# Element order of the PSUM copies of transposed q and k in a sparse-attention and mixture-of-experts kernel

## The chip, the core and the metric

The kernel runs on one core of a Trainium2 chip. The metric is the device time of one execution, in microseconds. A core has a matrix engine (TensorE, PE in the tables; its weight loads are listed as PEld), a vector engine (VectorE, DVE), an activation engine (ScalarE, ACT), GpSimd (POOL) and a queue for transfers (SyncE, SP). They run side by side and wait for one another through semaphores. PE writes its results to PSUM; DVE and ACT copy them from there to SBUF, from which PE reads its operands.

## The reference

Eight batches of eight heads, 576 positions, 64 features. Heads 0 to 3 see the 32 latest positions (local), heads 4 to 7 see the earlier positions that are equal modulo 32 (strided). The attention's output, as 4608 tokens of 512 features, goes through a top-1 mixture of eight experts with a capacity of 80 tokens.

```python
scores = scale * np.matmul(q, k.transpose(0, 1, 3, 2))
mask_local = (rel >= 0) & (rel < stride)                     # stride = 32
mask_strided = (rel >= 0) & (pos[None, :] % stride == pos[:, None] % stride)
scores = np.where(masks[None, :, :, :], scores, -1000000000.0)
attn = softmax(scores); attn_out = np.matmul(attn, v)
x = attn_out.transpose(0, 2, 1, 3).reshape(B * S, H * D)
expert_idx = np.argmax(x @ w_gate, axis=1)                   # gate_w: its probability
# of an expert's tokens the 80 with the largest gate are kept
h = np.maximum(x[tok_idx] @ w1[e], 0.0)
out[tok_idx] = gate_w[tok_idx, None] * (h @ w2[e])
```

## The kernel before

The attention takes up most of the first 235 us. Its work comes in 32 items: for each batch two of the local heads and two of the strided heads. In step i the kernel computes the scores of item i, the exponentials and their sums of item i-1, and the products with the values of item i-2. It transposes a q or a k for a later item, splits one chunk of expert weights into two float16 parts, and carries the previous batch's logits and rows of x on. So four steps make a batch. Each of these pieces is a generator, and `weave` takes their steps in an order that the table `WIN` sets. The instructions of each engine then stand in exactly that order: nothing is moved later by a scheduler, and an engine that waits holds up all that is queued behind it.

q and k arrive with nine positions side by side in a partition's row. PE transposes them in nine pieces of 128x128 (line 332), three to a PSUM tile `tp`; a piece j holds the positions 9 s + j. A copy per tile (two for k, one for each half of the partitions) puts them where the products read them: `qt` and `ktl` for local heads, `qs` and `kst` for strided ones, with positions in their natural order. Before the change the copy runs over pieces, then over positions of a piece, so that it reads PSUM without steps and writes every ninth float. The halves of `ktl` and `kst` that belong to other heads hold zeros, so that one product serves two.

Which engine makes a copy is told by the table `EV`, with "a" for ACT and "v" for DVE: the key `k01` is the middle tile of a local k, `k11` that of a strided k, `q..` those of q, all of them on ACT. In the profile the copies are lines 288 (ACT, plain), 290 (ACT, times a constant) and 292 (DVE).

For local items the weights (`pl`) are transposed (line 420), copied to `ptl` and multiplied with the values `vlo` (line 430). For strided items the weights `pr` become `pts`, and the products with the values (line 460) give a PSUM tile `o` with 288 columns, whose copy goes to `xr` (in the last batches to a part of `cp` or `raw`). There are two such copies an item, one per residue pair `rr`; before the change each holds all four heads of one residue and writes every fourth float. DVE reduces the scores' maxima (line 345), subtracts them (346), sums the exponentials that ACT makes (400, sums in 404) and takes half of the weight splits (211, after ACT's half in 210). GpSimd multiplies the weights by the reciprocal sums (407).

Of the kernel before, what the change touches and what calls it, by code (L numbers as in the profile page):

```python
# [20 lines left out]
P = 128  # L21
# [4 lines left out]
NTL = S // 32            # query tiles of a local head, 32 queries against 64 keys  # L26
NQ = 96                  # partitions of a batch's rows of x, 6 tokens each
NC6 = S // NQ
NSEG = 16                # segments of tokens in the routing, 8 experts each
NCAND = 16               # candidates kept of a segment and expert  # L30
SLOTS = 80               # tokens of an expert in the fast path
NEG = -1e30
FAR = 1000000.0
SC = 16.0                # scale of float16 parts
HALF = 4096              # a half of an expert's weights (w1 or w2), per partition
# [3 lines left out]
NR = 2                   # staged chunks during the attention  # L39
NST = 8                  # and after it  # L40
TL = ((0, 5), (5, 9))    # pairs of tiles of a local item
NPRE = 5                 # halves split during the attention
# [9 lines left out]
def moe_attention(ctx: ExitStack, tc, q, k, v, wg, w1, w2, cap, out):  # L52
# [3 lines left out]
    # rows of x by token id plus one; row 0 is zeros  # L56
    xs = dram.tile([NT + 1, DM], F32, name="xs")

# [8 lines left out]
    # additive masks; local: rows (head of the pair, tile parity, query), columns keys from 32 before the tile's  # L67
    # first query; strided: rows (head, block), columns blocks
    # their storage holds the routing's candidates later
# [32 lines left out]
    # column n of gates holds tokens 576 * (n // 6) + 6 * p + n % 6; chunk j of a partition's row of g288 holds column  # L102
    # 16 j + segment, so that position i of the row holds token 6 i + tb[j] - 1
# [6 lines left out]
    def attention_constants():  # L110
        nc.gpsimd.memset(mstr, 0.0)
        for g in range(4):
            m = mstr[32 * g:32 * g + 32]
            nc.gpsimd.affine_select(out=m, in_=m, pattern=[[0, 16], [-1, 18]], base=0, channel_multiplier=1,
                                    compare_op=ALU.is_ge, fill=NEG)
        for x in range(2):
            nc.gpsimd.memset(kst[64 * x:64 * x + 64, 1 - x], 0.0)
        # hm[p, z] = 1 where p // 18 == z
        nc.gpsimd.memset(hm, 1.0)
        nc.gpsimd.affine_select(out=hm, in_=hm, pattern=[[-18, 4]], base=0, channel_multiplier=1,  # L120
                                compare_op=ALU.is_ge, fill=0.0)
        nc.gpsimd.affine_select(out=hm, in_=hm, pattern=[[18, 4]], base=17, channel_multiplier=-1,
                                compare_op=ALU.is_ge, fill=0.0)
        # gate weights: columns (token parity, expert); strided heads have rows (token parity, d)
        nc.vector.memset(wgt, 0.0)
        for x in range(2):
            nc.sync.dma_start(wgl[:, x::2, E * x:E * x + E], wg[0:256].rearrange("(c p) e -> p c e", p=P))
            nc.sync.dma_start(wgs[64 * x:64 * x + 64, :, E * x:E * x + E],
                              wg[256:512].rearrange("(h d) e -> d h e", d=D))
        nc.gpsimd.iota(down_p, pattern=[[-1, E]], base=E, channel_multiplier=0, allow_small_or_imprecise_dtypes=True)  # L130
        # capacity on all partitions
        nc.sync.dma_start(capi, cap.broadcast_to([P, 2]))

    def routing_constants():
        # partition r = 8 * segment + expert; segm[r, s] = 1 where r // 8 == s
# [5 lines left out]
        # esel[r, e] = 1 where r % 8 == e  # L141
        nc.vector.tensor_reduce(esel, ident.rearrange("p (s e) -> p e s", e=E), op=ALU.add, axis=AX.X)
        # bon[r', r] = 1 where the experts agree; btr where also the segment of r' is the earlier
# [16 lines left out]
    # rows of q and k, zeros for the output and logits; later more staged chunks  # L160
    raw = wpool.tile([P, 4 * CH], F32, name="raw")
    # strided keys transposed, rows (parity, d) and for each parity a copy with the other's rows as zeros
# [10 lines left out]
    # the order in which the halves are used  # L173
# [12 lines left out]
    def wload(i):  # L186
        """Stages chunk i of the weights, 4 to a half."""
# [10 lines left out]
    def wsplit(pool=False):  # L198
        """The next staged chunk's weights, times SC, as the sum of two float16."""
# [35 lines left out]
    def warm(m):  # L235
        """Keeps the tensor engine's clock up while it has nothing to do."""
# [4 lines left out]
    # local keys transposed, rows (pair, d), columns (head of the pair, pair, position): of each pair's columns the  # L241
    # other pair's rows are zeros
    ktl = ap.tile([P, 2, 2, 32 + S], F32, name="ktl")
    # transposed weights; local: rows (pair, key), columns (pair of tiles, pair, (head of the pair, parity, query)): of
    # each pair's columns the other pair's rows are zeros
    ptl = ap.tile([P, 5, 2, P], F32, name="ptl")
    # values, rows (pair, key of the tile's 64), columns (tile, head of the pair, d)
# [11 lines left out]
    def loadv(st, m):  # L259
# [8 lines left out]
        else:  # L268
            # rows (quarter of the residues, block), columns (head, residue, d)
# [5 lines left out]
    def overlap(m, u):  # L275
        """The 32 keys before a tile."""
# [6 lines left out]
    def evac(kind, o, i, scale=None):  # L283
        """A copy that the table gives to an engine."""
# [11 lines left out]
    def interleave(st, which, first=False):  # L296
        """Rows of two local pairs of heads side by side."""
# [11 lines left out]
    def transposes(st, which):  # L309
        if st.g == 0:  # L310
            # rows (pair, d), columns (head of the pair, position)
# [7 lines left out]
        else:  # L319
            # rows (parity of the position, d), columns (head, half position)  # L320
# [7 lines left out]
        dvs = [d.rearrange("p h (s j) -> p j h s", j=9) for d in dvs]  # L328
        for j3 in range(3):
# [3 lines left out]
            tv = t.rearrange("p j (h s) -> p j h s", h=2 if st.g == 0 else 4)  # L333
            js = slice(3 * j3, 3 * j3 + 3)
            if which == 0:
                evac("q%d%d" % (st.g, j3), dvs[0][:, js], tv, 0.125)
            else:
                for x in range(2):
                    evac("k%d%d" % (st.g, j3), dvs[x][:, js], tv[64 * x:64 * x + 64])
# [9 lines left out]
    def scores(w, st, it):  # L349
# [3 lines left out]
        if st.g == 0:  # L353
            # rows (head of the pair, parity of the tile, query), columns (pair of tiles, pair, key)
# [21 lines left out]
        else:  # L376
            # rows (head, block), columns (residue pair, parity, quarter of the residues, block)
# [32 lines left out]
    def ptpv(w, xt):  # L410
        """Transposed weights times values: xt holds x transposed, local heads as (feature, position), strided
        heads as (parity of the position and d, (head, half position))."""
# [23 lines left out]
        else:  # L436
            # rows (quarter of the residues, block); for each quarter a copy with the others' rows as zeros
# [16 lines left out]
            for rr in range(2):  # L454
                o = ps_o.tile([P, 4, 4, 18], F32, name="o")
                r = 2 * it + rr
                for h2 in range(2):
                    for h in range(2 * h2, 2 * h2 + 2):
                        for x in range(2):
                            nc.tensor.matmul(o[64 * x:64 * x + 64, :, h], st.v[:, h, 2 * r + x],  # L460
                                             w.pt[:, :, 2 * rr + x, h], start=True, stop=True)
                    if h2 == 0:
                        yield
                evac("or%d" % it, xt[1].rearrange("p (h z r) -> p r z h", z=4, r=4)[:, r],
                     o.rearrange("p z h c -> p z (h c)"))
                yield

    def tail(b, xt):
        """Gates of the batch's tokens."""
# [31 lines left out]
        # of equal logits the first expert is taken  # L501
# [10 lines left out]
    def rows(b, xt):  # L512
        """The batch's rows of x to DRAM."""
# [26 lines left out]
    # buffers of the last batches' rows  # L540
# [4 lines left out]
    def xt_of(b, part):  # L545
        """x transposed of a batch: the last batches' are kept longer, where q and k are no longer needed."""
# [27 lines left out]
    def weave(*tasks):  # L574
        """Runs generators side by side; each is (generator, expected steps, start, end) with its share of the time."""
# [66 lines left out]
    for i in range(n + 2):  # L642
        gi, it = divmod(i, 2)
        tasks = []
        if i < n:
            wk[i] = St()
            tasks.append((scores(wk[i], stg[gi], it), (5 - it) if gi % 2 == 0 else 4, *WIN["s%d" % (i % 4)]))
            if i + 2 < n:
                # the last local q gives its place to x
# [15 lines left out]
        # batch b has its last item at 4 b + 3, worked on at step 4 b + 5  # L665
# [64 lines left out]
    # the largest gates of each segment  # L730
# [7 lines left out]
    # all candidates of an expert on each of its partitions  # L738
# [4 lines left out]
    # rows of x around the product  # L743
# [16 lines left out]
    # gate and token id (plus one) of each candidate, in bfloat16 parts, in the columns of its expert  # L760
# [20 lines left out]
    # the kept candidates are a prefix of the sorted row; its length by two steps of four  # L781
# [37 lines left out]
    # slot -> (token, gate) tables per expert  # L819
# [9 lines left out]
    # the gather reads row 0 where a slot is empty; the scatter skips it  # L829
# [26 lines left out]
    # the general path is taken when a segment may keep more tokens than it has candidates, or an expert more  # L856
    # than it has slots
# [119 lines left out]
    with tc.If(flag > 0):  # L977
        with tc.tile_pool(name="gp", bufs=1) as gp, tc.tile_pool(name="gw", bufs=1) as gw, \
# [70 lines left out]
          k01="v", k02="a", k10="a", k11="v", k12="a", pt0="a", pt1="v", pt2="a", o0="a", o1="a", o2="a", or0="a",  # L1049
# [46 lines left out]
```

## Time and profile before

| what | us |
|---|---|
| median of 3 runs | 340.87 |
| lowest and highest run | 337.51, 343.25 |
| span of the profiled execution, first to last instruction | 336.3 |
| PE busy in the span | 292.0 |
| ACT busy in the span | 260.0 |
| DVE busy in the span | 258.6 |

For the profiled execution only its span is known, not a time of its own; durations below come from it. Busy times are sums over the whole span. Waits are listed as the time that an engine stood idle before an instruction, with the instruction that released it.

### The profile page before, as it was taken

The page shows a single profiled execution, that of the slowest core. Times are in us where ns is not written, and L with a number is a line of the kernel's source. Part 1 is how long each engine was busy: PE and PEld are TensorE (multiplying, and loading weights), DVE is VectorE, ACT ScalarE, POOL GpSimd, SP SyncE. Part 2 cuts the span into 40 slices and gives each one's busy share as a digit, 9 for nine tenths or more (in the row PEclk, how much of TensorE's full clock was granted, in tenths as well). Part 3 has the DMA queues.
Part 4 walks back from the last instruction along what each step waited for, and adds up shares of the span by engine and source line. Part 5 has one row for each costly group of instructions (what it writes and reads, how often), then busy time and mean ns, then how long its engine had stood idle before and what let it go on. Part 6 is the DMA issues. An engine that isn't in the chain of part 4 may idle for free. (4 is left out here: it accounts for less than half of the span.)

```text
span 336.3 us, 12495 instructions
## 1 busy us (share of the span) xinstructions
PE 292.0 (87%) x5248; PEld 225.5 (67%) x5248; DVE 258.6 (77%) x513; ACT 260.0 (77%) x411; POOL 122.0 (36%) x151
## 2 busy tenths in 40 slices
PE   7588988999899899899989889989775997889892
PEld 7356556766566676666656565677675997889891
DVE  5466589789888978988978575778685899879860
ACT  3697898998899799889989868752544797779761
POOL 8853551363055146116405523420046243111112
PEclk9799999999999999999989999999997899999998
DMA  8969449789969969998898999769699899999801
GB/s 245 240 170 324 157 127 306 169 239 247 260 183 260 294 157 307 233 217 233 260 313 243 322 284 299 200 203 306 202 308 294 268 345 361 405 362 300 311 25 43
DMA packets 56527, 84.25 MB, mean 251 GB/s; under 512 B 23442, under 2 KB 32660, under 8 KB 56468
## 3 DMA queue, kind: packets, MB, share of 16 engines
q1 hardware_dynamic: 55444, 80.79, 80.3%
q0 software_dynamic: 1024, 2.62, 2.5%
q8 instruction: 43, 0.70, 0.9%
q14 instruction: 16, 0.13, 0.1%
HBM read 63.21 MB, written 20.19 MB: 248 GB/s over the span
## 5 line engine op out<-in xcount | busy, mean ns | idle before, releaser
L211 DVE SCALAR_TENSOR_TENSOR spl<-ring,spl 128x1024 f16<-128x1024 f32 x32 | 48.3, 1519 | 9.9 <-ACT spl L210 9.9
L899 PEld LDWEIGHTS <-spl 128*128 128x128 f16 x512 | 51.6, 101 | 3.2 <-issue 3.2
L897 PEld LDWEIGHTS <-spl 128*128 128x128 f16 x512 | 51.6, 101 | 2.7 <-issue 2.6
L898 PEld LDWEIGHTS <-spl 128*128 128x128 f16 x512 | 51.6, 101 | 2.4 <-issue 2.2
L278 POOL TENSOR_SCALAR vlo<-vlo 32x1152 f32<-32x1152 f32 (+1 forms) x32 | 39.3, 1227 | 2.6
L407 POOL TENSOR_TENSOR pr<-pr,sm 128x288 f32<-128x288 f32 (+1 forms) x17 | 11.0, 645 | 77.3 <-DVE sm L406 57.5
L430 PE MATMUL o<-ptl,vlo 128*64 128x64 f32 x576 | 30.2, 234 | 9.8 <-ACT ptl L288 9.6
L288 ACT COPY ktl<-tp 64x384 f32<-64x384 f32 (+1 forms) x40 | 32.1, 815 | 8.3 <-PE tp L332 7.2
L210 ACT ACTIVATE spl<-ring 128x1024 f16<-128x1024 f32 x32 | 33.5, 1060 | 4.2 <-DVE oh L823 4.2
L407 POOL TENSOR_TENSOR pl<-pl,sm 128x640 f32<-128x640 f32 (+1 forms) x16 | 18.5, 1155 | 45.9 <-DVE sm L406 30.1
L430 PEld LDWEIGHTS o<-ptl,vlo 128*64 128x64 f32 x576 | 22.8, 140 | 18.1 <-ACT ptl L288 13.0
L897 PE MATMUL hp<-xe,spl 128*128 128x80 f16 x256 | 31.0, 205 | 2.5 <-issue 1.9
L899 PE MATMUL hp<-xe,spl 128*128 128x80 f16 x256 | 30.9, 205 | 1.4 <-issue 1.4
L387 PE MATMUL s<-kst,qs 128*18 128x36 f32 x1024 | 30.9, 253 | 1.0 <-issue 1.0
L369 PE MATMUL s<-ktl,qt 128*32 128x128 f32 x576 | 28.0, 290 | 3.8 <-ACT ktl L288 3.8
L460 PE MATMUL o<-pts,vs 72*64 72x72 f32 x512 | 29.0, 237 | 2.6 <-DVE pts L446 2.5
L898 PE MATMUL hp<-xe,spl 128*128 128x80 f16 x256 | 30.9, 205 | 0.3 <-DVE xe L892 0.3
L288 ACT COPY kst<-tp 64x384 f32<-64x384 f32 x32 | 27.7, 865 | 2.7 <-PE tp L332 2.4
L898 PE MATMUL yp<-he,spl 128*128 128x80 f16 x256 | 28.6, 202 | 1.1 <-issue 1.1
L899 PE MATMUL yp<-he,spl 128*128 128x80 f16 x256 | 28.6, 202 | 1.1 <-issue 1.1
L460 PEld LDWEIGHTS o<-pts,vs 72*64 72x64 f32 x512 | 20.4, 135 | 13.5 <-issue 7.3
L897 PE MATMUL yp<-he,spl 128*128 128x80 f16 x256 | 28.6, 202 | 0.6 <-issue 0.6
(211 smaller groups left out, 758.2 us busy)
## 6 DMA issues: line engine op xcount, KB each, us to landing
ring<-moe_w SPq DMA_DIRECT2D x32, 512.0 KB
raw<-moe_w SPq DMA_DIRECT2D x21, 512.0 KB
raw<-q SPq DMA_DIRECT2D x16, 576.0 KB
raw<-k SPq DMA_DIRECT2D x16, 576.0 KB
out<-raw SPq DMA_DIRECT2D x18, 512.0 KB
kst<-moe_w SPq DMA_DIRECT2D x11, 512.0 KB
vs<-v SPq DMA_DIRECT2D x32, 144.0 KB
xs<-xn SPq DMA_DIRECT2D x12, 384.0 KB
```

The source lines that it names most:

```text
L210: nc.scalar.activation(hi, r, AF.Copy, scale=SC)
L211: nc.vector.scalar_tensor_tensor(lo, r, SC, hi, op0=ALU.mult, op1=ALU.subtract)
L278: nc.gpsimd.tensor_scalar(vlo[64 * u:64 * u + 32, t0:t1], vlo[64 * u + 32:64 * u + 64, t0 - 1:t1 - 1], 1.0, 0.0, op0=ALU.mult, op1=ALU.add)
L288: nc.scalar.copy(o, i)
L369: nc.tensor.matmul(s[32 * g:32 * g + 32, 128 * c:128 * c + 128], st.qt[:, h, k0:k0 + 32], ktl[:, h, :, k0:k0 + 64], start=False, stop=(c = ...
L387: nc.tensor.matmul(so[32 * h:32 * h + 18, rr, :, z], st.qt[:, h, r::16], kst[:, :, h, r::16], start=False, stop=(rr == 1 and z == 3), tile ...
L407: nc.gpsimd.tensor_tensor(pv, pv, sm[:, a:z].unsqueeze(2).broadcast_to([P, z - a, nk]), op=ALU.mult)
L430: nc.tensor.matmul(o[64 * h:64 * h + 64, :, k0:k0 + 32], vlo[:, 2 * (t0 + c) + x, h], ptl[:, c, :, 32 * g:32 * g + 32], start=True, stop=True)
L460: nc.tensor.matmul(o[64 * x:64 * x + 64, :, h], st.v[:, h, 2 * r + x], w.pt[:, :, 2 * rr + x, h], start=True, stop=True)
L897: nc.tensor.matmul(o, w[:, 0, i:i + P], x[:, 0, c], start=first, stop=False)
L898: nc.tensor.matmul(o, w[:, 0, i:i + P], x[:, 1, c], start=False, stop=False)
L899: nc.tensor.matmul(o, w[:, 1, i:i + P], x[:, 0, c], start=False, stop=last)
```

## The change

The copies of q and k run over positions first and over the three pieces of a tile last: they write runs of three neighbouring floats, every nine floats, and read the three from pieces 128 floats apart in PSUM. The copies of the strided results take two residues of two heads in place of one residue of four heads: they write pairs of neighbouring floats, every four floats, and read the two 36 floats apart. For this the products of the strided heads fill the tile `o` in another order. `k01` goes from DVE to ACT. All else in the diff is comments.

```diff
-        dvs = [d.rearrange("p h (s j) -> p j h s", j=9) for d in dvs]
+        dvs = [d.rearrange("p h (s j) -> p h s j", j=9) for d in dvs]
         for j3 in range(3):
             t = ps_t.tile([P, 3, P], F32, name="tp")
             for jj in range(3):
                 nc.tensor.transpose(t[:, jj], cp[:, 3 * j3 + jj], ident)
-            tv = t.rearrange("p j (h s) -> p j h s", h=2 if st.g == 0 else 4)
+            tv = t.rearrange("p j (h s) -> p h s j", h=2 if st.g == 0 else 4)
             js = slice(3 * j3, 3 * j3 + 3)
             if which == 0:
-                evac("q%d%d" % (st.g, j3), dvs[0][:, js], tv, 0.125)
+                evac("q%d%d" % (st.g, j3), dvs[0][:, :, :, js], tv, 0.125)
             else:
                 for x in range(2):
-                    evac("k%d%d" % (st.g, j3), dvs[x][:, js], tv[64 * x:64 * x + 64])
+                    evac("k%d%d" % (st.g, j3), dvs[x][:, :, :, js], tv[64 * x:64 * x + 64])
             yield
...
-            for rr in range(2):
-                o = ps_o.tile([P, 4, 4, 18], F32, name="o")
-                r = 2 * it + rr
-                for h2 in range(2):
-                    for h in range(2 * h2, 2 * h2 + 2):
+            for h2 in range(2):
+                o = ps_o.tile([P, 4, 2, 2, 18], F32, name="o")
+                for rr in range(2):
+                    for hh in range(2):
                         for x in range(2):
-                            nc.tensor.matmul(o[64 * x:64 * x + 64, :, h], st.v[:, h, 2 * r + x],
+                            h = 2 * h2 + hh
+                            nc.tensor.matmul(o[64 * x:64 * x + 64, :, rr, hh], st.v[:, h, 2 * (2 * it + rr) + x],
                                              w.pt[:, :, 2 * rr + x, h], start=True, stop=True)
-                    if h2 == 0:
+                    if rr == 0:
                         yield
-                evac("or%d" % it, xt[1].rearrange("p (h z r) -> p r z h", z=4, r=4)[:, r],
-                     o.rearrange("p z h c -> p z (h c)"))
+                evac("or%d" % it, xt[1].rearrange("p (c z r) -> p z c r", z=4, r=4)[:, :, 36 * h2:36 * h2 + 36,
+                                                                                    2 * it:2 * it + 2],
+                     o.rearrange("p z r h c -> p z (h c) r"))
                 yield
...
-          k01="v", k02="a", k10="a", k11="v", k12="a", ...
+          k01="a", k02="a", k10="a", k11="v", k12="a", ...
```

The rows of PE, GpSimd and the transfer queue keep their order. On ACT and DVE only the local k copies of `k01` move. This is ACT in the last step of a batch's cycle, before the change; `ex` belongs to the logits, `xl` and `xn` to results, `spl` to a weight split:

```order
L210 ACTIVATE spl_129<-ring_124 128x1024
L288 COPY xl<-o 128x2x192
L290 ACTIVATE qt<-tp 128x3x128
L499 ACTIVATE ex<-ex 96x48
L288 COPY xl<-o 128x2x128
L288 COPY ktl<-tp 64x3x2x64 x2
L288 COPY ptl<-tp 64x4x128 x2
L400 ACTIVATE pr<-pr 128x288
L288 COPY ktl<-tp 64x3x2x64 x2
L288 COPY xn<-tp 96x2x256
L210 ACTIVATE spl_129<-ring_123 128x1024
```

and the same place after it:

```order
L210 ACTIVATE spl_129<-ring_124 128x1024
L288 COPY xl<-o 128x2x192
L290 ACTIVATE qt<-tp 128x128x3
L502 ACTIVATE ex<-ex 96x48
L288 COPY xl<-o 128x2x128
L288 COPY ktl<-tp 64x2x64x3 x2
L288 COPY ptl<-tp 64x4x128 x2
L401 ACTIVATE pr<-pr 128x288
L288 COPY ktl<-tp 64x2x64x3 x4
L288 COPY xn<-tp 96x2x256
L210 ACTIVATE spl_129<-ring_123 128x1024
```

Two `ktl` copies have come in behind the exponential of `pr`, next to the two that stood there. On DVE this is the same stretch before the change, from the maxima of an item's scores on:

```order
L345 TENSOR_REDUCE mx<-s 128x16
L346 TENSOR_TENSOR pr<-s,mx 128x288
L292 COPY xn<-tp 96x2x256
L292 COPY ktl<-tp 64x3x2x64 x2
L404 TENSOR_REDUCE sm<-pr 128x16
L405 TENSOR_SCALAR sm<-sm 128x16
```

and after it:

```order
L346 TENSOR_REDUCE mx<-s 128x16
L347 TENSOR_TENSOR pr<-s,mx 128x288
L292 COPY xn<-tp 96x2x256
L405 TENSOR_REDUCE sm<-pr 128x16
L406 TENSOR_SCALAR sm<-sm 128x16
```

The two copies have left DVE's queue between the copy to `xn` and the sum of `pr`. Two `kst` and two `qt` copies stand on ACT earlier in the same step, ahead of the first row shown here; before the change:

```order
L288 COPY kst<-tp 64x3x128 x2
L290 ACTIVATE qt<-tp 128x3x128
L288 COPY ptl<-tp 64x3x128 x2
L400 ACTIVATE pl<-pl 128x512
L481 COPY raw<-tp 128x288
L290 ACTIVATE qt<-tp 128x3x128
```

and after it, in the same order and with the other form of copy:

```order
L288 COPY kst<-tp 64x128x3 x2
L290 ACTIVATE qt<-tp 128x128x3
L288 COPY ptl<-tp 64x3x128 x2
L401 ACTIVATE pl<-pl 128x512
L484 COPY raw<-tp 128x288
L290 ACTIVATE qt<-tp 128x128x3
```

Only the last two numbers of a form have changed places there; nothing has moved.

## Rows read from the trace of the kernel before

**Rows 1.** The page: busy time, share of the span, instructions of each engine.

```profile
PE 292.0 (87%) x5248; PEld 225.5 (67%) x5248; DVE 258.6 (77%) x513; ACT 260.0 (77%) x411; POOL 122.0 (36%) x151
```

**Rows 2.** Stretches of the span: length, busy time of each engine, clock, DMA.

```profile
core 0: us, PE busy (x) PEld busy (x) DVE busy (x) ACT busy (x) POOL busy (x), PEclk, DMA share, GB/s
25.00:215.00 190.00, 174.85 (x2935) 120.78 (x2931) 153.32 (x311) 167.52 (x271) 76.09 (x76) 0.99 0.87 245
125.00:150.00 25.00, 23.32 (x399) 16.11 (x398) 22.12 (x43) 22.47 (x38) 8.31 (x8) 1.00 0.96 253
```

**Rows 3.** PE's waits from 25 to 215: releaser, us in total, times, longest.

```profile
PE o L430 <- ACT ptl L288: 8.3, 13, 1.3
PE o L460 <- DVE pts L446: 2.5, 7, 1.0
...
PE tp L474 <- ACT qt L290: 0.3, 1, 0.3
```

**Rows 4.** Waits of PE's weight loads in the same stretch.

```profile
PEld o L430 <- ACT ptl L288: 11.0, 13, 1.5
...
PEld tp L332 <- DMA raw<-q: 0.2, 1, 0.2
```

**Rows 5.** PE's timeline: start, length, instruction, idle time before it and its releaser.

```profile
12.57 0.65 PE L369 MATMUL s<-ktl,qt 128*32 128x128 f32 x16 [3.23 <-ACT ktl L288]
...
86.48 0.52 PE L430 MATMUL o<-ptl,vlo 128*64 128x64 f32 x8 [1.24 <-ACT ptl L288]
...
111.29 0.60 PE L420 MATMUL tp<-ident,pl 128*128 128x128 f32 x4
...
113.27 0.48 PE L387 MATMUL s<-kst,qs 128*18 128x36 f32 x16
115.02 0.52 PE L430 MATMUL o<-ptl,vlo 128*64 128x64 f32 x8 [1.27 <-ACT ptl L288]
```

**Rows 6.** ACT's timeline, at the start and around 111 to 118.

```profile
7.01 2.26 ACT L290 ACTIVATE qt<-tp 128x384 f32<-128x384 f32 x3 [4.92 <-PE tp L332]
9.06 3.45 ACT L288 COPY ktl<-tp 64x384 f32<-64x384 f32 x4
...
111.56 0.24 ACT L499 ACTIVATE ex<-ex 96x48 f32<-96x48 f32 x1 [0.84 <-DVE ex L498]
...
111.96 1.80 ACT L288 COPY ktl<-tp 64x384 f32<-64x384 f32 x2
113.78 1.18 ACT L288 COPY ptl<-tp 64x512 f32<-64x512 f32 x2
...
116.47 1.74 ACT L288 COPY ktl<-tp 64x384 f32<-64x384 f32 x2 [1.03 <-PE tp L332]
```

**Rows 7.** Groups from 0 to 240: busy us, mean ns of one, idle before.

```profile
L288 ACT COPY ktl<-tp 64x384 f32<-64x384 f32 x32 | 27.9, 871 | 7.6 <-PE tp L332 7.2
L290 ACT ACTIVATE qt<-tp 128x384 f32<-128x384 f32 x24 | 21.1, 914 | 5.1 <-PE tp L332 4.9
L288 ACT COPY xr<-o 128x288 f32<-128x288 f32 x24 | 16.3, 678 | 1.6 <-PE o L460 1.4
L292 DVE COPY ktl<-tp 64x384 f32<-64x384 f32 x16 | 13.7, 854 | 0.8 <-PE tp L332 0.7
L288 ACT COPY ptl<-tp 64x384 f32<-64x384 f32 x16 | 8.1, 509 | 0.2
L346 DVE TENSOR_TENSOR pl<-s,mx 128x384 f32<-128x384 f32 x8 | 4.5, 558 | 0.8
L481 ACT COPY raw<-tp 128x288 f32<-128x288 f32 x8 | 3.3, 409 | 4.5 <-PE tp L479 4.3
```

**Rows 8.** The same view: two reductions of DVE that read PSUM.

```profile
L345 DVE TENSOR_REDUCE mx<-s 128x4 f32<-128x256 f32 x8 | 3.4, 420 | 1.3 <-PE s L369 1.2
...
L488 DVE TENSOR_REDUCE lg<-tp 96x48 f32<-96x192 f32 x8 | 2.8, 354 | 2.1 <-PE tp L487 1.9
```

**Rows 9.** DVE's timeline: a weight split.

```profile
109.55 1.62 DVE L211 SCALAR_TENSOR_TENSOR spl<-ring,spl 128x1024 f16<-128x1024 f32 x1 [0.30 <-ACT spl L210]
```

More of the change, by code (lines that the diff above doesn't have):

```diff
@@ L1048 @@
 EV = dict(cp="p", x0="v", x1="a", y="a", ys="a", q00="a", q01="a", q02="a", q10="a", q11="a", q12="a", k00="a",
-          k01="v", k02="a", k10="a", k11="v", k12="a", pt0="a", pt1="v", pt2="a", o0="a", o1="a", o2="a", or0="a",
+          k01="a", k02="a", k10="a", k11="v", k12="a", pt0="a", pt1="v", pt2="a", o0="a", o1="a", o2="a", or0="a",
           or1="a", ps0="a", ps1="v")
```

## The prediction

> **What bounds the kernel now.** I read the page first: TensorE (PE) is busy 87% of the span, VectorE (DVE) and ScalarE (ACT) 77% each [rows 1], a mean over stages. The edits lie in the attention, so the table of stretches comes next: from 25 to 215 us PE is busy 174.85 of 190 us, ACT 167.52, DVE 153.32 [rows 2]. Three engines stand near their limit, so what counts is who makes whom wait. PE's waits in this stretch fill eight rows, 15.1 us, which is its idle time (190 - 174.85). Five of them end with ACT and sum to 10.7 us, the first with 8.3 and the last with 0.3; one ends with DVE, 2.5 [rows 3]; GpSimd has 0.9, and 1.0 has no releaser. So PE is the bound, and ACT is what starves it. PE's weight loads, which feel a wait earlier, name ACT's ptl copies too, with 11.0 us [rows 4].
>
> The timelines show why. Batches repeat: the same wait for ptl ends at 86.48 and at 115.02, 28.5 us apart [rows 5]. PE has done what was queued at 113.75 (113.27 + 0.48) and stands until 115.02 for the ptl copies, whose transposes ended at 111.89 (111.29 + 0.60) [rows 5]. ACT could not start them: it ran two ktl copies from 111.96 to 113.76 and ptl after them, to 114.96 [rows 6]. These ktl copies are among those that the change edits.
>
> **The price of one copy.** Every copy of q and k moves 384 elements of a partition, side by side in PSUM, to every ninth float of SBUF: 871 ns on ACT for k, 914 for q, 854 on DVE. ACT moves a 64x384 tile into runs without steps (ptl) in 509 ns [rows 7]. A lone write thus costs (871 - 509) / 384 = 0.94 ns more. The strided results agree: to every fourth float, 678 ns against 409 for 288 elements without steps [rows 7], 269 / 288 = 0.93. On DVE 854 stands against 558 for an operation on 384 elements without steps [rows 7], 0.77 ns an element.
>
> No row shows runs of three or of two, so bounds: at best they cost like runs without steps (509), at worst like lone writes (871). I let each run pay once what a lone write pays: 128 runs x 0.94 = 121, 630 ns for a k copy, a saving of 241, and the same saving for q. That is nearer to 509, because two of three writes follow their neighbour. A pair copy has 144 runs, 409 + 144 x 0.93 = 543, a saving of 135. On DVE 558 + 128 x 0.77 = 657, a saving of 197.
>
> The Trainium skill (SBUF — State Buffer, Specifications) says that SBUF has lines of 16 bytes, needs two hits on a line for full bandwidth, and pays for each cross to a new one. The rows of lone writes agree (871 against 509 ns). By it two of four runs of three lie within one line and two leave one float alone in another: 64 lone writes in place of 128, an estimate of 570 ns for the k copy where the sum takes 630, which would take some 1 us a batch more off ACT.
>
> **The reads.** The new copies also step through PSUM, 512 bytes between the three elements of a run. The nearest row is a reduction on DVE (line 488) whose inner step in PSUM is 128 bytes: 354 ns for 192 elements, where one without steps takes 420 for 256 [rows 8]. That lies between 315 (420 x 192 / 256) and 420, as plain reads would; 0.77 ns more an element would give 463 or more. Stepped reads cost DVE nothing. ACT has no such row. I take nothing for it, and keep the whole saving as the other end (rival 3).
>
> **The sums on each engine.** ACT: 48 q copies and 64 k copies x 0.241 = 27.0 us less; 28 pair copies (24 to xr, 4 of the same size to cp) x 0.135 = 3.8 less. The table also moves the 16 middle local k copies from DVE to ACT: 16 x 0.630 = 10.1 more. Net 20.7 us less, 2.6 a batch; bounds 112 x 0.362 + 28 x 0.269 - 16 x 0.509 = 39.9 less, and 16 x 0.871 = 13.9 more. DVE: 16 x 0.854 = 13.7 less for the moved copies, 16 x 0.197 = 3.2 for its strided k copies, 4 x 0.135 = 0.5 for its pair copies: 17.4 less, 2.2 a batch.
>
> The instructions of PE, GpSimd and the DMA queue keep their order and count. The result products of the strided heads take the heads in another order, eight before each copy as now, into outputs of the same size; this costs nothing by itself.
>
> **Where the moved copies go.** On ACT they stand behind the exponential of pr and ahead of the last two ktl copies, and these are followed by a copy to xn and a weight split. There ACT waits 1.03 us for PE's transposes [rows 6]; those of the moved pair stand on PE ahead of its row at 113.27 [rows 5] and are long done. Of 2 x 0.630 = 1.26 us, 1.03 lies in this wait and 0.23 on ACT's path. Without that cover the copies would cost 1.26 a batch, 10 us in all. On DVE they leave the place ahead of the sum of pr, for which GpSimd's product waits.
>
> **What it is worth.** At the wait of 115.02 the two ktl copies are shorter by 0.48 us. Ahead of them ACT waited for DVE until 111.56 [rows 6]; DVE came there from a weight split at 109.55, and that had waited for ACT [rows 9], which in this step ran two kst and two qt copies ahead of it (4 x 0.24 = 0.96 us). So up to 1.4 us of delay goes where PE waits 1.27, while PE itself arrives earlier as its other waits shrink. I give three quarters of the 13.2 us that PE waits for ACT and DVE: 9.9 us. The last quarter stays, since the copies still stand between transposes and product. Next late is PE's own work, 174.85 us of 190.
>
> At the start PE waits 3.23 us until 12.57 for the first ktl copies [rows 5]. ACT copies q from 7.01 and k until 12.51 [rows 6]. New: 2.26 - 3 x 0.241 = 1.54 us for q, then six k copies in place of four, 3.78 us: 12.33, 0.2 us earlier (1.0 if a copy costs 509). After 215 us only few of these copies are left, and I count nothing there. Routing and experts keep their length.
>
> Sum: 9.9 + 0.2 = 10.1 us. Of the profiled execution only the span is given, 336.3 us; the nearest timed run, 337.51, lies 1.2 above it, the median, 340.87, 4.6. Off the median 10.1 us leave 330.8, say **331 us**. The runs spread 0.85% to either side; 2%, some 7 us, is about what a measurement of this kernel tells from no change.
>
> **Rival 1, more.** If runs cost 509 ns, ACT loses 40 us: all 13.2 us of PE's waits go, and 1.0 at the start: 326.7. By the weight loads' waits for ACT and DVE, 23.7 us in fourteen rows, the first 11.0 [rows 4], it could reach 316. For it: those loads feel waits that PE's busy time hides behind the ends of earlier products. Against: PE's own work does not shrink.
>
> **Rival 2, another end.** The DMA engines are 0.96 busy from 125 to 150 us [rows 2]. If transfers keep their time whatever the engines do, such a batch shrinks by at most 4% of 28.5 us, 1.1 us, and by half of that as a mean over eight: some 4 us, 337. For it: that share. Against: in 190 us PE's loads wait for a transfer once, 0.2 us [rows 4].
>
> **Rival 3, slower.** ACT's stepped reads cost what the lone writes did, and a copy stays at 871 ns. Then the 16 moved copies put 1.74 us a batch more on ACT in the place above; 1.03 lie in ACT's wait, 0.71 do not: 8 x 0.71 = 5.7 us, at most all 13.9. That is 347 to 355; the low end is likelier, since the wait is there in each batch. It decides from 13.9 / 128 = 109 ns: if a copy saves less than that, and so costs over 762, ACT gains nothing. For it: no row shows ACT reading so. Against: DVE's reduction [rows 8].
>
> The Trainium skill (Advanced Engine Details and Errata, Memory Cachelines) speaks for rival 3: PSUM has lines of 8 bytes, and every two elements in a row should be contiguous for best throughput. The reduction above differs from it for DVE; no row here shows it for ACT.
>
> **How the numbers follow.** Forecast 0.60, 326 to 336 (half of PE's waits for ACT and DVE gone gives 334.1, all of them 327.5); rival 1 beyond that 0.12, 316 to 326; rival 2 0.15, 334 to 341; rival 3 0.13, 345 to 355. The range, 320 to 343, leaves out the lower half of rival 1 and all of rival 3, some 0.19. Faster by 2% is below 334: 0.54 of the forecast's 0.60 and rival 1, 0.66. Within 2%: 0.06 + 0.15 + 0.02 of rival 3, 0.23. Slower: 0.11.
>
> **What would show it.** Right: k copies on ACT at 540 to 690 ns; PE's waits for ptl at a quarter of 8.3 us; batches of 27.2 us. Wrong: copies over 762 ns; or cheap copies with batches of 28 us or more, and PE's waits passed on to transfers, GpSimd's products or DVE. If ACT waits for PE where PE waited for ACT, PE's work is the last bound.

## The result and the profile after

The changed kernel takes 325.74 us (324.52 to 326.72, 4 runs), the kernel before 339.19 (4 runs); the ratio is 0.9609, 95% interval 0.9553 to 0.9665. That is 13.4 us less, where the prediction had 10.1. The ratios here and below compare undisturbed executions alone while the medians take in all, so the quotient of two medians can differ from the ratio by up to half a per cent.

The page of the changed kernel, busy time and share (before: [rows 1]):

```profile
PE 291.8 (90%) x5248; PEld 225.8 (70%) x5248; DVE 236.7 (73%) x497; ACT 235.4 (73%) x427; POOL 123.4 (38%) x151
```

ACT lost 24.6 us of work, DVE 21.9; PE works as long as before, in a span 11.6 us shorter. The costs of one copy, as groups of the changed kernel from 0 to 235 us (before: [rows 7]):

```profile
L288 ACT COPY ktl<-tp 64x384 f32<-64x384 f32 x48 | 26.7, 556 | 1.8 <-PE tp L333 0.9
L288 ACT COPY kst<-tp 64x384 f32<-64x384 f32 x32 | 17.6, 550 | 8.5 <-PE tp L333 7.9
L290 ACT ACTIVATE qt<-tp 128x384 f32<-128x384 f32 x24 | 13.3, 578 | 5.1 <-PE tp L333 4.9
L288 ACT COPY xr<-o 128x288 f32<-128x288 f32 x24 | 9.8, 407 | 5.1 <-PE o L462 4.9
L292 DVE COPY kst<-tp 64x384 f32<-64x384 f32 x16 | 9.0, 560 | 5.5 <-PE tp L333 5.3
```

A k copy went from 871 to 556 ns, a q copy from 914 to 578, a pair copy from 678 to 407, which is what 288 elements without steps cost [rows 7]. The same attention stage, as a stretch of the changed kernel, and one inside a steady batch (before: [rows 2]):

```profile
core 0: us, PE busy (x) PEld busy (x) DVE busy (x) ACT busy (x) POOL busy (x), PEclk, DMA share, GB/s
24.50:204.00 179.50, 173.29 (x2937) 120.00 (x2935) 134.11 (x296) 146.47 (x286) 80.10 (x76) 0.99 0.91 260
100.00:125.00 25.00, 24.68 (x413) 17.43 (x409) 19.90 (x43) 21.28 (x42) 10.28 (x11) 1.00 0.92 257
```

PE is busy 24.68 of 25 us, while ACT and DVE now have room. PE's waits in that stage (before: [rows 3]):

```profile
PE o L462 <- DVE pts L447: 1.9, 6, 0.9
PE s L388 <- issue: 1.3, 1, 1.3
PE o L431 <- ACT ptl L288: 1.2, 2, 0.6
...
PE o L462 <- ACT pts L452: 0.4, 1, 0.4
```

ACT and DVE end 3.5 us of them, where they ended 13.2. The wait for ptl fell from 8.3 us in 13 places to 1.2 in two. A batch is marked by the products for its logits, on PE's timeline of the changed kernel:

```profile
70.43 0.71 PE L477 MATMUL tp<-xl,wgt 128*32 128x288 f32 x8
...
97.17 0.71 PE L477 MATMUL tp<-xl,wgt 128*32 128x288 f32 x8
```

26.74 us apart, where the same marks of the kernel before stood 28.5 apart. At the place of [rows 5] and [rows 6], ACT's timeline of the changed kernel reads:

```profile
103.74 0.24 ACT L502 ACTIVATE ex<-ex 96x48 f32<-96x48 f32 x1 [0.97 <-DVE ex L501]
103.89 0.35 ACT L288 COPY xl<-o 128x256 f32<-128x256 f32 x1
104.26 1.13 ACT L288 COPY ktl<-tp 64x384 f32<-64x384 f32 x2
105.41 1.20 ACT L288 COPY ptl<-tp 64x512 f32<-64x512 f32 x2
106.64 0.44 ACT L401 ACTIVATE pr<-pr 128x288 f32<-128x288 f32 x1
107.10 2.28 ACT L288 COPY ktl<-tp 64x384 f32<-64x384 f32 x4
```

and PE's:

```profile
104.06 0.60 PE L421 MATMUL tp<-ident,pl 128*128 128x128 f32 x4
...
106.04 0.48 PE L388 MATMUL s<-kst,qs 128*18 128x36 f32 x16
106.66 0.52 PE L431 MATMUL o<-ptl,vlo 128*64 128x64 f32 x8
```

The ktl pair takes 1.13 us in place of 1.80, ptl ends at 106.61, and PE, done at 106.52 (106.04 + 0.48) with what stood ahead, goes on at 106.66 without a wait that the view lists. It still starts only 0.05 us after ptl has ended, so the two now arrive almost together. Behind it four ktl copies run back to back: ACT's wait of 1.03 us is gone, filled by the two that were moved.

The first maximum of the routing's gates marks the end of the attention: 241.75 us before, 228.03 after. So 13.7 us were gained ahead of it. Behind it the program took 94.55 and 96.67 us, at a mean granted clock of 0.95 and 0.91. The other profiled executions below spread from 92.6 to 96.5 us there, so I do not put these 2 us down to the change.

### The profile page after: what moved, and what is told of

It reads as the page before. It is cut to its first block, busy times and chain, and to the rows that moved or that the text cites. A ratio compares the mean times of both kernels' runs of the same rounds, so it can differ in the third digit from the quotient of the medians.

```text
span 324.7 us, 12487 instructions
## 1 busy us (share of the span) xinstructions
PE 291.8 (90%) x5248; PEld 225.8 (70%) x5248; DVE 236.7 (73%) x497; ACT 235.4 (73%) x427; POOL 123.4 (38%) x151
## 5 line engine op out<-in xcount | busy, mean ns | idle before, releaser
L901 PEld LDWEIGHTS <-spl 128*128 128x128 f16 x512 | 52.1, 102 | 3.1 <-issue 2.9
L900 PEld LDWEIGHTS <-spl 128*128 128x128 f16 x512 | 52.2, 102 | 2.9 <-issue 2.9
L902 PEld LDWEIGHTS <-spl 128*128 128x128 f16 x512 | 52.1, 102 | 1.9 <-issue 1.9
L211 DVE SCALAR_TENSOR_TENSOR spl<-ring,spl 128x1024 f16<-128x1024 f32 x32 | 44.2, 1388 | 5.8 <-ACT spl L210 4.4
L278 POOL TENSOR_SCALAR vlo<-vlo 32x1152 f32<-32x1152 f32 (+1 forms) x32 | 40.2, 1257 | 4.6 <-DMA vlo<-v 2.3
L900 PE MATMUL hp<-xe,spl 128*128 128x80 f16 x256 | 32.0, 208 | 1.6 <-issue 1.0
L902 PE MATMUL hp<-xe,spl 128*128 128x80 f16 x256 | 31.9, 208 | 1.4 <-issue 1.4
L901 PE MATMUL hp<-xe,spl 128*128 128x80 f16 x256 | 31.9, 207 | 1.2 <-issue 0.9
L288 ACT COPY ktl<-tp 64x384 f32<-64x384 f32 (+1 forms) x56 | 30.9, 561 | 2.5 <-PE tp L333 0.9
L431 PE MATMUL o<-ptl,vlo 128*64 128x64 f32 x576 | 28.8, 230 | 2.3 <-ACT ptl L288 1.7
L462 PEld LDWEIGHTS o<-pts,vs 72*64 72x64 f32 x512 | 20.4, 136 | 13.4 <-issue 8.9
L346 DVE TENSOR_REDUCE mx<-s 128x16 f32<-128x288 f32 (+3 forms) x40 | 20.2, 504 | 12.0 <-PE s L370 5.9
L431 PEld LDWEIGHTS o<-ptl,vlo 128*64 128x64 f32 x576 | 21.7, 137 | 9.9 <-ACT ptl L288 3.9
```

Of the source, the lines that this page charges most:

```text
L211: nc.vector.scalar_tensor_tensor(lo, r, SC, hi, op0=ALU.mult, op1=ALU.subtract)
L278: nc.gpsimd.tensor_scalar(vlo[64 * u:64 * u + 32, t0:t1], vlo[64 * u + 32:64 * u + 64, t0 - 1:t1 - 1], 1.0, 0.0, op0=ALU.mult, op1=ALU.add)
L288: nc.scalar.copy(o, i)
L431: nc.tensor.matmul(o[64 * h:64 * h + 64, :, k0:k0 + 32], vlo[:, 2 * (t0 + c) + x, h], ptl[:, c, :, 32 * g:32 * g + 32], start=True, stop=True)
L462: nc.tensor.matmul(o[64 * x:64 * x + 64, :, rr, hh], st.v[:, h, 2 * (2 * it + rr) + x], w.pt[:, :, 2 * rr + x, h], start=True, stop=True)
L900: nc.tensor.matmul(o, w[:, 0, i:i + P], x[:, 0, c], start=first, stop=False)
```

## Experiments

**Which part pays.** In what follows, threes are the copies that write runs of three, pairs those that write runs of two, and the move is that of `k01`. My theory was that cheaper copies on ACT let PE run without waits. The rivals were that DVE's relief by the moved copies pays, or that the pairs do. First the change with `k01` back on DVE:

```diff
-          k01="a", k02="a", ...
+          k01="v", k02="a", ...
```

> The changed kernel with k01 on DVE again: threes and pairs, nothing moved. Theory (cheaper copies on ACT let PE run without waits; the move adds nothing): PE is dense in the changed kernel already, so the time stays within 1.5 us of it, 324 to 327 (ratio to before 0.956 to 0.965), with ACT 16 x 0.556 = 8.9 us lighter and DVE 16 x 0.56 = 9 us heavier. Rival (the gain comes from relieving DVE by the moved copies): half or more of the 13 us is lost, 331 or more.

Measured: 326.14 us, ratio 0.9656 (0.9596 to 0.9715), an interval that overlaps with the change's own. The move adds nothing that can be measured. Then the move alone, the same edit the other way on the kernel before:

```diff
-          k01="v", k02="a", ...
+          k01="a", k02="a", ...
```

> The kernel before with k01 on ACT and nothing else: lone writes everywhere. Theory: ACT gets 16 x 0.871 = 13.9 us more, 1.74 a batch, of which its wait of 1.03 covers a part: 4 to 14 us slower, 343 to 353 (ratio 1.012 to 1.04). Rival (DVE's relief is what pays): faster, 331 to 336.

Measured: 344.01, ratio 1.0171 (1.0117 to 1.0224), by the ratio 5.8 us slower. DVE's relief by 14 us buys nothing, and ACT's 14 us more cost time: this is the case of rival 3 with copies that stayed dear, whose low end was 5.7. The cost does not lie in longer waits for ptl, which sum to 9.6 us over the whole span here and in the kernel before. A steady batch takes 29.0 us in place of 28.5, 0.5 more where 0.71 were forecast, and the start is later, which rival 3 did not count. ACT's copies there:

```profile
8.90 5.14 ACT L288 COPY ktl<-tp 64x384 f32<-64x384 f32 x6
```

Six long copies end at 14.04, and PE's first scores begin at 14.19 where they began at 12.57 [rows 5].

The change without the pairs (the old products and copies of the strided results):

```diff
-            for h2 in range(2):
-                o = ps_o.tile([P, 4, 2, 2, 18], F32, name="o")
+            for rr in range(2):
+                o = ps_o.tile([P, 4, 4, 18], F32, name="o")
...
```

> The changed kernel with the strided results' copies and products as before: threes and the move, no pairs. Theory: 28 copies go back from 0.41 to 0.68 us, 7.6 us more on ACT, which waits 4.9 us for PE ahead of just these copies now: 0 to 3 us slower than the changed kernel, 325 to 329 (ratio 0.96 to 0.97). Rival (pairs carry half of the gain): 331 to 333.

Measured: 325.30, ratio 0.9624 (0.9567 to 0.9680): all of the gain. Threes without the move and without the pairs were not run together; each was taken away singly and nothing was lost. And the pairs alone, the opposite edit on the kernel before:

```diff
-            for rr in range(2):
-                o = ps_o.tile([P, 4, 4, 18], F32, name="o")
+            for h2 in range(2):
+                o = ps_o.tile([P, 4, 2, 2, 18], F32, name="o")
...
```

> The kernel before with the pairs only. Theory: ACT gets 7.6 us lighter, 0.95 a batch, in the strided items, while the wait that costs most (1.27 us for ptl) lies behind the ktl copies: 1 to 4 us faster, 335 to 338 (ratio 0.988 to 0.997). Rival (pairs carry half): 331 to 333 (0.98).

Measured: 340.09, ratio 0.9998 (0.9952 to 1.0044): nothing, less than the 1 to 4 us that I expected. The copies did get cheaper. A group of that run, and PE's wait at the place of 115.02 [rows 5]:

```profile
L288 ACT COPY xr<-o 128x288 f32<-128x288 f32 x24 | 10.4, 435 | 2.4 <-PE o L460 2.3
```

```profile
87.62 0.52 PE L430 MATMUL o<-ptl,vlo 128*64 128x64 f32 x8 [1.36 <-ACT ptl L288]
```

ACT is 3 us less busy (256.7), and ACT's idle time ahead of these copies, while PE makes their products, grew from 1.6 to 2.4 us. The wait for ptl stands at 1.36 us where it was 1.27, and the steady batches at 28.57 and 28.48 us where they were 28.5. Over the whole span the waits of these products come to 9.2 us where they came to 9.6: 6.7 are put down to ptl, and 2.5, at two of the same places, to transfers. Time saved on ACT was worth nothing here, where it did not shorten the wait for ptl.

**The price of a copy by itself.** Ahead of the changed kernel, 13 forms of a 64x384 copy from PSUM, four of each, on each engine; `runs(step, off, n)` writes n neighbours every `step` floats from `off`, `s3` and `s2` read the neighbours 128 and 192 floats apart. Shown are lines 80, 84 (the change), 86, 90, 92, 94 and 96 of that kernel:

```diff
+            for _ in range(4):
+                cp_(d[:, 0:384], s)
...
+                cp_(runs(9, 0, 3), s3)
...
+                cp_(d[:, 0:384].rearrange("p (s j) -> p s j", j=3), s3)
...
+                cp_(runs(8, 0, 3), s3)
...
+                cp_(runs(8, 2, 3), s3)
...
+                cp_(runs(4, 0, 2), s2)
...
+                cp_(runs(4, 3, 2), s2)
...
```

> The changed kernel with 13 forms of a 64x384 copy from PSUM ahead of it, four of each, on ACT and then on DVE; only their own durations count. Theory A (a write is dear where it is the only one in its 16 bytes): on ACT without steps about 510 ns, lone writes at steps of 9, 4 floats 870, step 3 about 690 (two of four alone), step 2 about 510; threes every 9 floats 550 to 570 with stepped and with plain reads alike; stepped reads into plain writes 510; threes every 8 floats 510 from offset 0 and 630 from offset 2 (one of three crosses into the next 16 bytes); pairs every 4 floats 510 from offset 0, 870 from offset 3. Theory B (each run of neighbours pays once, wherever it lies): threes 550 to 560 in all three placements, pairs alike from offset 0 and 3, steps of 2 and 3 as dear as 9. Rival (stepped reads of PSUM cost): stepped reads into plain writes well over 510.

Measured, as the durations (least, median, most) of these lines; 82 is the form before the change, 88 writes threes from plain reads, 98 to 104 write lone floats at steps of 2, 3, 4 and 9:

```profile
L80 ACT COPY md<-mp x4: 472/472/472, 2.2 to 3.7; 64x384 f32<-64x384 f32 x4
L82 ACT COPY md<-mp x4: 832/832/837, 4.2 to 6.8; 64x384 f32<-64x384 f32 x4
L84 ACT COPY md<-mp x4: 539/540/542, 7.7 to 9.4; 64x384 f32<-64x384 f32 x4
L86 ACT COPY md<-mp x4: 472/472/472, 10.0 to 11.5; 64x384 f32<-64x384 f32 x4
L88 ACT COPY md<-mp x4: 539/546/552, 12.0 to 13.7; 64x384 f32<-64x384 f32 x4
L90 ACT COPY md<-mp x4: 472/472/473, 14.3 to 15.8; 64x384 f32<-64x384 f32 x4
L92 ACT COPY md<-mp x4: 600/600/602, 16.3 to 18.2; 64x384 f32<-64x384 f32 x4
L96 ACT COPY md<-mp x4: 491/496/501, 20.9 to 22.5; 64x384 f32<-64x384 f32 x4
L98 ACT COPY md<-mp x4: 492/494/495, 23.0 to 24.6; 64x384 f32<-64x384 f32 x4
L100 ACT COPY md<-mp x4: 657/662/662, 25.1 to 27.2; 64x384 f32<-64x384 f32 x4
L102 ACT COPY md<-mp x4: 823/824/824, 27.9 to 30.5; 64x384 f32<-64x384 f32 x4
```

```profile
L80 DVE COPY md<-mp x4: 549/549/550, 2.6 to 4.4; 64x384 f32<-64x384 f32 x4
L82 DVE COPY md<-mp x4: 829/830/835, 4.9 to 7.5; 64x384 f32<-64x384 f32 x4
L84 DVE COPY md<-mp x4: 550/552/552, 8.4 to 10.2; 64x384 f32<-64x384 f32 x4
L86 DVE COPY md<-mp x4: 549/550/551, 10.8 to 12.5; 64x384 f32<-64x384 f32 x4
L92 DVE COPY md<-mp x4: 598/599/599, 17.8 to 19.7; 64x384 f32<-64x384 f32 x4
L100 DVE COPY md<-mp x4: 653/654/655, 27.3 to 29.4; 64x384 f32<-64x384 f32 x4
```

Stepped reads of PSUM cost nothing on ACT, be it into plain writes (line 86 against 80) or into threes (84 against 88): rival 3's premise is false. Writes follow theory A. A lone write costs (832 - 472) / 384 = 0.94 ns more. Counting floats that are written alone in their 16 bytes: threes every nine have 64, 472 + 60 = 532, measured 540; threes every eight from offset 2 have 128, 592, measured 600; from offset 0 none, 472; step 3 has 192, 652, measured 662. Theory B has the three placements of threes alike, and they are not. One of my expectations under theory A was wrong by its own rule: pairs from offset 3 cost 496 and not 870, because the second of a pair and the first of the next lie in the same 16 bytes and are written one after the other. On DVE, whose plain copy takes longer (549 against 472), threes every nine cost nothing extra (552); more lone floats do, but less than 0.94 ns each (599 with 128 of them, line 92; 654 with 192, line 100).

**Is PE the bound?** One of three transposes of q and k made twice, in both kernels:

```diff
                 nc.tensor.transpose(t[:, jj], cp[:, 3 * j3 + jj], ident)
+                if jj == 0:
+                    nc.tensor.transpose(t[:, jj], cp[:, 3 * j3 + jj], ident)
```

> The changed kernel with one of three transposes of q and k made twice, 96 more on PE; three back to back take 0.38 us there, so 12 us of PE work, and nothing for the other engines. Theory (PE is the bound after the change): 11 to 15 us slower than the changed kernel, 337 to 341 (ratio to before 0.995 to 1.005). Rival (another chain sets the pace): under 6 us, below 332.

> The kernel before with the same 96 transposes more. Theory (PE stands 13 us waiting for ACT and DVE, so added work fills part of that): 4 to 9 us slower, 343 to 348 (ratio 1.012 to 1.027), less than in the changed kernel. Rival (PE was as much the bound before): the same 11 to 15 us, 350 or more.

Measured: 329.65 (0.9713, 0.9673 to 0.9752) and 343.60 (1.0146, 1.0099 to 1.0194). The kernel before lost 4.6 us, within the 4 to 9 forecast. The changed one lost only 3.9 where 11 to 15 were forecast: by that expectation's own words its rival, that another chain sets the pace, came true. The added transposes stand 0.11 us apart in the trace, 10.6 us in all and not 12. By batches the two differ: the changed kernel's steady batch grows from 26.74 to 27.85 us, 1.11 for 12 x 0.11 = 1.32 us of added work, the other's from 28.5 to 28.9. In the two profiled executions of the changed kernel the attention ends 5.9 us later with the load, not 8 x 1.1. In part that is one batch: without the load the fifth batch between marks took 28.15 us, 2.1 of it idle time of PE that has no releaser, at a granted clock of 0.94; with the load it took 26.30 at 1.00. The rest I did not find. So the load was made three times as large, every transpose twice:

```diff
-                nc.tensor.transpose(t[:, jj], cp[:, 3 * j3 + jj], ident)
+                for _ in range(2):
+                    nc.tensor.transpose(t[:, jj], cp[:, 3 * j3 + jj], ident)
```

> The changed kernel with every transpose of q and k made twice: 288 more on PE, 0.11 us each where they stand back to back, 32 us, 4.0 a batch. Theory (PE is the bound after the change, a few tenths of a batch are left): 25 to 32 us slower than the changed kernel, 350 to 358 (ratio to before 1.035 to 1.055). Rival (96 more transposes cost it only 4 us of 10.6, so other chains hold it as much): 12 to 15 us slower, 338 to 341 (1.00).

> The kernel before with the same 288 transposes more. Theory (PE's added work fills its waits for ACT, 2.2 us a batch, before it costs; then both kernels are bound by PE alike): 15 to 22 us slower than the kernel before, 354 to 361 (1.045 to 1.065), at most 6 us above the changed kernel with the same load, where 13 lie between the two now. Rival (waits are passed on, not filled): the distance stays at 13 us.

Measured: 348.28 (1.0197, 1.0110 to 1.0284) and 354.12 (1.0402, 1.0322 to 1.0483). The changed kernel loses 20 (by the ratios) to 22.5 us (by the medians), under my 25 to 32 and well over the rival's 12 to 15; the kernel before loses 14.4 against its 339.77, just under 15 to 22. The distance falls from 13.4 us to 6 by the medians and 7 by the ratios, close to the 6 expected of waits that are filled. The stretch from 50 to 150 us of the changed kernel with this load, and of the kernel before with it:

```profile
50.00:150.00 100.00, 99.45 (x1581) 74.33 (x1581) 69.02 (x157) 77.71 (x147) 37.69 (x32) 1.00 0.84 231
```

```profile
50.00:150.00 100.00, 98.69 (x1564) 73.17 (x1565) 78.74 (x159) 87.38 (x138) 35.55 (x32) 1.00 0.82 226
```

Both have PE at 99%. Steady batches take 30.2 and 30.7 us, and most of these 0.6 us is the wait for ptl, now 0.42 to 0.47 us a batch in the kernel before:

```profile
91.74 0.52 PE L431 MATMUL o<-ptl,vlo 128*64 128x64 f32 x8 [0.47 <-ACT ptl L288]
```

**Place or sum?** In the prediction the ktl pair right ahead of ptl and the copies further ahead both delayed PE. Two runs with threes in one part of the copies (`lone` picks the old order of axes), first in the local k alone:

```diff
+        lone = not (st.g == 0 and which == 1)
+        dvs = [d.rearrange("p h (s j) -> p j h s" if lone else "p h (s j) -> p h s j", j=9) for d in dvs]
...
```

> The changed kernel with threes in the copies of the local k alone; q and the strided k are written as before, pairs and the move stay. Theory (the wait of 1.27 us a batch behind the ktl copies, and ACT's delay ahead of it): ktl is shorter by 0.63 us for a pair there, but kst and qt still delay what stands ahead, 7 to 10 of the 13 us remain gained: 329 to 332 (ratio 0.97 to 0.98). Rival (it is ACT's sum, wherever it is saved): ACT saves 64 of 128 copies' worth less the moved copies, about a third of the gain, 334 to 336.

then in all but the local k:

```diff
+        lone = st.g == 0 and which == 1
...
```

> The counterpart of the run with threes in the local k alone: q and the strided k write threes, all 48 local k copies on ACT write lone floats as before; pairs and the move stay. Theory (the place of the copies counts, the ktl pair right ahead of ptl above all): ACT is some 10 us lighter than in the kernel before, yet PE's wait of about 1.2 us for ptl stays in each batch: 335 to 339 (ratio 0.99 to 1.00). Rival (ACT's sum counts, wherever it is saved): half of the 13 us is gained, 331 to 334 (0.975 to 0.985).

Measured: 332.79 (0.9834, 0.9791 to 0.9877) and 335.71 (0.9846, 0.9784 to 0.9908). The first lies between its two forecasts, 329 to 332 and 334 to 336. The second lies at the edge of both, in the theory's range by time (335 to 339) and in the rival's by ratio (0.975 to 0.985). PE's wait at the place of 115.02, with the local k alone:

```profile
85.13 0.52 PE L432 MATMUL o<-ptl,vlo 128*64 128x64 f32 x8 [0.68 <-ACT ptl L288]
```

and with all but the local k:

```profile
87.85 0.52 PE L432 MATMUL o<-ptl,vlo 128*64 128x64 f32 x8 [0.76 <-ACT ptl L288]
```

1.27 us fell to 0.68 by the shorter pair and to 0.76 by what is ahead, and is not listed when both are shorter. A steady batch takes 27.8 to 27.9 us in both, some 0.65 less than 28.5 each, where both together take 1.8 off. The second gains less as a whole because its start is later: six local k copies that are still long end at 13.16 us, PE's first scores begin at 13.30 in place of 12.57, and the first batch's mark stands at 49.57, where with the local k alone it stands at 46.78. Neither pure theory stands: it looks as if the delay in ACT's queue is a sum along the chain to ptl, and either part of the copies alone brings less than half of what both bring in a batch. The sum over all of ACT is not the measure either: with the local k alone ACT is busy 256.0 us, with all but the local k 249.5, and the lighter one gains no more. With the pairs alone it is busy 256.7 and gains nothing (the move is in the first two only; alone it costs time).

The last run was to take 21 us off ACT in another way. It is the kernel before with ACT's half of the 20 weight splits during the attention given to GpSimd:

```diff
-            nc.scalar.activation(hi, r, AF.Copy, scale=SC)
+            if i < NCH * NPRE:
+                nc.gpsimd.tensor_scalar(hi, r, SC, 0.0, op0=ALU.mult, op1=ALU.add)
+            else:
+                nc.scalar.activation(hi, r, AF.Copy, scale=SC)
```

> The kernel before with ACT's half of the 20 weight splits during the attention given to GpSimd, which is busy 76 of 190 us: ACT 21 us lighter, as much as the prediction's sum took off it, with all copies as before. Theory (the place counts; the split stands ahead of the copies that PE waits for, but the ktl pair ahead of ptl stays at 1.8 us): 2 to 6 us faster, 333 to 337 (0.982 to 0.994). Rival A (ACT's sum counts): 10 us faster, 328 to 331. Rival B (GpSimd's products of the weights come later behind the splits): slower.

Measured: 349.13, ratio 1.0240 (1.0172 to 1.0307), slower. ACT is 14 us less busy (245.8), not 21, and PE waits longer for it. In the kernel before, ACT's wait for the logits was this, from 25 to 215 us:

```profile
ACT ex L499 <- DVE ex L498: 4.6, 6, 0.8
```

Waits of this run in the same stretch, where PE's for ptl was 8.3 us before [rows 3]:

```profile
ACT ex L502 <- DVE ex L501: 14.3, 6, 3.0
DVE spl L214 <- POOL spl L211: 13.0, 8, 2.0
...
PE o L433 <- ACT ptl L291: 14.5, 12, 2.9
```

This is not rival B's chain (products of the weights) but the one named in the prediction at 109.55: DVE's split waits for its first half, now GpSimd's, the logits stand behind that split, ACT's `ex` waits for them, and ktl and ptl stand behind `ex`. PE itself also ran slower: from 50 to 150 us its granted clock was 0.95, where it was 1.00 before, and it was busy 88.99 us of these 100 while it waited; how much of the loss is the clock's is not shown.

## Why the prediction was right

The time, 325.74, lies 0.3 us below the forecast's own range, 326 to 336, and so in that of rival 1; direction and mechanism held as forecast. Of the 5 us between 331 and the result, 1.7 are the base: the 10.1 us were taken off a median of three runs, 340.87, where the four give 339.19. The other 3.3 are gain that the sum did not have. Point by point:

- **The bound.** PE waited for ACT; its waits for ACT and DVE in the stage fell by 9.7 us, where 9.9 were forecast. With doubled transposes the two kernels come within 6 to 7 us of each other, so PE's work is what is late next for the most part; the smaller load does not bear that out.
- **The price of a copy** was the term most off. I took 630 ns for threes and 543 for pairs, one lone write's price a run; measured are 556 and 407. Only floats that are alone in their 16 bytes pay. The Trainium skill (SBUF — State Buffer, Specifications) has the rule of two hits to a line of 16 bytes, and the trace agrees (472 ns where no float is alone, line 90; 600 where one of three is, line 92). The estimate of 570 by it was the nearer one.
- **ACT's sum** was put at 20.7 us less; it is 24.6. DVE's was put at 17.4; it is 21.9, and some 4 of it are its weight splits, 1388 ns each in place of 1519, which no term had.
- **The reads** cost nothing, as taken from DVE's reduction [rows 8]; line 86 shows it for ACT. The other rule of the Trainium skill that I weighed, contiguous pairs in PSUM (Advanced Engine Details and Errata, Memory Cachelines), does not hold for reads by ACT and DVE here: 472 ns against 472 and 550 against 549 (line 86 against 80).
- **The moved copies.** Their cover was named rightly: ACT's wait of 1.03 us took them, at 0.57 us each. Undoing the move costs nothing measurable, while without cheap copies it costs 5.8 us.
- **Three quarters.** Over the stage the share was right, 9.7 of 13.2 us. It is not even: in a steady batch PE's idle time fell from 1.9 us (1.69 of 25 in the stretch from 100, scaled to 28.5) to 0.34, five sixths, and the batches take 26.74 us and not 27.2.
- **Where the rest lies.** In the profiles 13.7 us were gained up to the first maximum, 3.6 more than the sum. By the start of the same product of PE, 24.94 before and 22.99 after, 1.95 us of them were gained ahead of 25 us, where 0.2 were counted. From there to 215 the stage is 10.5 us shorter, where 9.9 were counted. Behind 215, where nothing was counted, 1.3 more were gained.
- **The start.** PE's first scores began at 11.77 in place of 12.57, because six copies cost 3.32 and not 3.78 us and those of q 1.43. The sum had also laid the copies of q and k end to end, where [rows 6] have k begin 0.21 us before q ends. At the other end of that term, 1.0 us, only the k copies were put at 509 ns; with q at its lower price too the sum gives 1.3.
- **The pairs** were counted into ACT's sum and bring nothing by themselves.
- Rival 2 did not come: at 0.88 to 0.96 of DMA the steady batches shrank all the same. In rival 1 the weight loads' waits for ACT and DVE are 23.9 us in fifteen rows, not 23.7 in fourteen, which moves that rival by 0.2 us.

Still open is why 96 added transposes cost the changed kernel only 3.9 us as a whole, when its steady batches say more.

## What to carry to other kernels

Price a strided write by where it lands: count the elements that find no neighbour, written just before or after, in their 16 bytes, and choose the loop order so that few are left; a stepped read from PSUM was free here. Then ask which copies stand in a queue ahead of one that the busiest engine waits for: 3 to 4 us taken off ACT gained 6 us in one place (with the copies moved) and nothing in another. A lighter engine was no gain where the work went to an engine whose result that queue waits for.

## What the runs showed of the hardware that I had not expected

Two writes need not belong to one run: pairs at an odd offset (496 ns) and floats at a step of two (494) cost nearly what plain writes do (472), and a step of three (662) lies half way to a step of four (824). DVE hides threes at a step of nine altogether (552 against 549), where ACT pays 68 ns, but not threes that all leave one float alone (599). A step of 512 bytes between reads of PSUM is free on both engines (472 against 472, 550 against 549).
